# One batch's pieces reordered between another's channel products, its value casts moved to GpSimd, and three batches' numerators placed a step earlier (attention and MLP mixer)

## The chip, the cores and the metric

One core of a Trainium2 chip runs the whole kernel. The metric is the device time of one execution in microseconds (us); the time of a version is the median of its runs.

## The reference

Eight batches of eight heads, 576 positions, 64 features per head. Linear attention with cosine and sine weights is followed by a mixer that has a token part and a channel part:

```python
q_p, k_p = phi(q, cos_w, sin_w), phi(k, cos_w, sin_w)   # relu(x)*cos, relu(x)*sin
kv  = einsum('bhsf,bhsd->bhfd', k_p, v)
num = einsum('bhsf,bhfd->bhsd', q_p, kv)
den = einsum('bhsf,bhf->bhs', q_p, sum_s(k_p))[..., None] + 1e-06
x   = num / den                                         # heads side by side: (8, 576, 512)
h   = relu(x^T @ w_tok1) @ w_tok2                       # token part
u   = x + h^T
out = u + relu(u @ w_ch1) @ w_ch2                       # channel part
```

## The kernel before

**Tiles.** The 576 positions of a batch are four chunks of 128 (numbers 0 to 3) and a tail of 64; the tails of an even and the next odd batch share one tile of 128 partitions (`Tail`). `R` is 4, so "chunk `R`" is the tail; `NCH` is 12, the blocks of the hidden channel width.

**Two parts of a batch.** `Front` computes everything up to `u`, `Channel` the channel part. The order is written out by hand (manual schedule): each engine runs its instructions in the order in which the Python code issues them, and waits on semaphores where data or a buffer is missing. The channel part of batch b is a list of steps: 12 steps `c` (a block of `u @ w_ch1`, four matmuls of 512 columns; slots 0 to 11, from `C` = 0), then steps of two matmuls each for `o` (the product with `w_ch2`; slots from `O` = 12). Behind each step, `pieces` puts pieces of the front part of batch b+1, by a plan of (slot, function, arguments); within a slot they run in the order of the plan. So TensorE's own stream is: a step, some pieces, a step, some pieces.

**The pieces.** `KS` and `QS` (k_side, q_side) make the cosine and the sine product of a chunk of keys or queries (line 264 on VectorE; with `True` the sine goes to ScalarE, line 262). `QT` (q_trans) turns a chunk of queries on TensorE (line 343, eight transposes into a PSUM tile of pool `ps_at`, which has two buffers) and copies it out on ScalarE (line 347) or VectorE (line 349); later batches turn by DMA instead (line 353). `V` (values, line 267) casts a chunk of values to bf16 into `v_aug`. `KV` (line 321) multiplies keys and values of a chunk into `kv_ps` (one `ps_at` buffer), `kv_out` (line 332) copies the sum out, one half on ScalarE and the other on VectorE. `N` (num, line 362, `num_ps` in `ps_at`) gives numerator and denominator of a chunk; three VectorE instructions divide. `mix_head` and `mix_tail` are the first token product (line 385, relu at lines 390 and 392), `T` (tok2) is the second (line 409) with the addition that makes `u` (line 412) and its cast (lines 414, 416). `u_trans_dma` and `tail_trans_dma` turn `u` by DMA from SP's queue (lines 438, 443) for the next channel part. Stores of finished outputs are issued from SP too (line 571).

**The first two batches.** The front part of batch 0 (`first_front`) runs alone. The channel part of batch 0 starts before batch 0's `u` has been added up, so the five `tok2` calls of batch 0 (`before.tok2`) are among the pieces of batch 1. Batch 1's plan has its own branch (`first`) and ends in one long slot 11, in which the rest of its front work up to `kv_out` is issued between the last `c` and the first `o`.

**Loads.** SP issues all loads of queries, keys and values in a written order; GpSimd issues the weights `w_ch1` and `w_ch2` (line 194).

Of the kernel before, what the change touches and what calls it, by code (L numbers as in the profile page):

```python
# [16 lines left out]
def kernel(  # L17
# [15 lines left out]
    nc = tc.nc  # L33

    B, H, S, D = q.shape
# [5 lines left out]
    R = S // P  # L41
    SM = R * P
    ST = S - SM
    NSC = R + 1
    NCC = Dm // P
    NT = D_tok // P
    NCH = D_ch // P
# [9 lines left out]
    def half(g):  # L57
        return slice(g * ST, (g + 1) * ST)
# [14 lines left out]
    ps_at = ctx.enter_context(tc.tile_pool(name="ps_at", bufs=2, space=bass.MemoryType.PSUM))  # L73
# [14 lines left out]
            in_=src[b, lo:hi, 0:SM, :].rearrange("h (p r) d -> p h r d", r=R))  # L88


    def load_tail(dst, src, b):
        return nc.sync.dma_start(out=dst[half(b % 2)],
                                 in_=src[b, :, SM:S, :].rearrange("h s d -> s h d"))

    def tiles():
# [8 lines left out]
    load_main(qt0, q, 0, 0, HH)  # L104
    load_main(qt0, q, 0, HH, H, nc.scalar)
    load_tail(qtt0, q, 0)
    load_main(kt0, k, 0, 0, HH)
    k_done = load_main(kt0, k, 0, HH, H)
    load_tail(ktt0, k, 0)
    load_main(vt0, v, 0, 0, HH)  # L110
    load_tail(vtt0, v, 0)
    load_main(vt0, v, 0, HH, H)

# [72 lines left out]
    for c2 in range(2):  # L186
        for ki in range(0, NCC, 2):
            w_ch1_done.append(nc.gpsimd.dma_start(
                out=w_ch1[:, ki:ki + 2, c2 * C2:(c2 + 1) * C2],
# [27 lines left out]
    class Front:  # L217
# [243 lines left out]
        def pieces(self, b, before):  # L461


            first, odd = b == 1, b % 2 == 1
            V, KV, N = self.values, self.kv, self.num
            KS, QS, QT, T = self.k_side, self.q_side, self.q_trans, self.tok2
            C, O = 0, NCH
            if first:

                last = NCH - 1  # L470
                plan = [(4, KS, 0), (5, KS, 1, True), (6, KS, 2, True), (6, KS, 3, True), (7, KS, R),
                        (8, QS, 0), (9, QS, 1), (9, QT, 0), (10, QS, 2), (10, QT, 1)]
                plan += [(last, *what) for what in (
                    (QS, 3, True), (QT, 2, (0, H), nc.vector), (before.tok2, 2, None, False),
                    (QS, R, True), (QT, 3), (before.tok2, 3, None, False),
                    (QT, R, (0, H), nc.vector), (before.tok2, R, None, False))]
                plan += [(last, V, ci, eng) for ci, eng in enumerate(
                    (nc.gpsimd, nc.gpsimd, nc.scalar, nc.scalar, nc.vector))]
                plan += [(last, KV, ci) for ci in range(NSC)]
                plan.append((last, self.kv_out))  # L480
                plan += [(5, before.tok2, 0, ps_at, False), (7, before.tok2, 1, ps_at, False)]
            else:
                plan = [(C + at, V, ci, nc.scalar) for ci, at in enumerate((-1, -1, 0, 1, 2))]
                plan += [(C + at, KS, ci) for ci, at in enumerate((0, 0, 1, 2, 2))
                         if ci < R or not odd]
                for ci, at in zip(ORDER, (1, 2, 3, 4, 5)):
                    if ci < R or not odd:
                        plan += [(C + at, QS, ci), (C + at, self.q_trans_dma, ci)]

                plan += [(C + at, KV, ci) for ci, at in  # L490
                         enumerate((2, 3, 4, 5, 6) if odd else (2, 3, 4, 6, 7))]
                plan.append((C + (6 if odd else 7), self.kv_out))
            if first:
                at, mix, t = (O + 1, O + 3, O + 5, O + 7, O + 9), O + 10, O + 14
            elif odd:
                at, mix, t = (C + 8, C + 9, C + 11, O + 1, O + 3), O + 4, O + 8
            else:
                at, mix, t = (C + 9, C + 10, C + 11, O + 1, O + 3), O + 4, O + 8
            plan += [(i, N, ci) for i, ci in zip(at, ORDER)]
            plan += [(mix, self.mix_head, 0), (mix + 1, self.mix_head, 1),  # L500
                     (mix + 2, self.mix_tail)]

            plan += [(t + at, T, ci) for ci, at in enumerate((0, 1, 2, 3, 3) if not first else
                                                             (0, 0, 1, 2, 2))]
            plan += [(t + 3 - first, self.u_trans_dma, 3, R)]
            plan.append((t + 2 - first, self.u_trans_dma, 0, 3))
            if odd:
                plan.append((t + 3 - first, self.tail_trans_dma))
            slots = {}
            for slot, what, *args in sorted(plan, key=lambda p: p[0]):  # L510
                slots.setdefault(slot, []).append((what, args))
            return slots
# [269 lines left out]
```

## Time and profile before

| | us |
|---|---|
| median of 3 runs (276.20 to 278.07) | 277.34 |
| profiled execution, device time | 275.45 |
| its span (first to last instruction) | 273.60 |
| TensorE busy in the span | 261.6 |
| VectorE, ScalarE, GpSimd busy | 164.7, 129.8, 11.2 |

The profile is of one execution. "Busy" of TensorE is modelled from the matmuls' starts; a matmul of 512 columns is listed with 372 ns, but the next one starts 216 ns after it (24 of them start between 24.10 and 29.28 us), so 216 ns is what one costs where TensorE is never idle. A "wait" is idle time of an engine in front of an instruction, with the engine or transfer that ended it. A time with a colon or without a unit is a place in the span, in us from its start. The granted TensorE clock is 1.00 over the whole span.

By time, the span falls into the lone front part of batch 0 (0 to 24), the channel part of batch 0 with batch 1's pieces (24 to 60), then one channel part of about 30 us per batch, and the last one alone (from 244).

### The profile page before, as it was taken

What the parts mean: (1) busy time and instruction counts of PE and PEld (TensorE: products, weight loads), DVE (VectorE), ACT (ScalarE), POOL (GpSimd) and SP (SyncE); (2) the same over time, 40 slices, a digit from 0 to 9 for tenths busy, and PEclk for the clock granted to TensorE, in tenths of its full rate; (3) what the DMA queues carried; (4) which work ended last, traced back from release to release, by engine and by line L of the source; (5) the groups of instructions that cost most, each with busy time, mean ns of one, the idle gap of its engine ahead of it and who ended that gap; (6) DMA issues with size and microseconds to landing.
All of it is one profiled execution on the core that took longest, in us unless ns stands there. A gap on an engine that the chain in (4) does not pass through costs nothing.

```text
span 273.6 us, 5130 instructions
## 1 busy us (share of the span) xinstructions
PE 261.6 (96%) x2050; PEld 138.7 (51%) x2050; DVE 164.7 (60%) x375; ACT 129.8 (47%) x229; POOL 11.2 (4%) x24
## 2 busy tenths in 40 slices
PE   7989987999899999999999999999999999999994
PEld 2665354446554454445654455446644455435543
DVE  6973775774876396659566487659466577720022
ACT  4955982067525184156626183347606372426500
POOL 6400230000000000000000000000000000000000
PEclk9999999999999999999999999999999999999999
DMA  7999999738995897968993969669994361180032
GB/s 222 344 266 283 317 179 283 245 88 264 284 253 185 247 221 191 323 140 233 208 311 79 270 193 259 220 151 237 211 304 119 115 117 38 42 210 0 2 98 94
DMA packets 91816, 53.68 MB, mean 196 GB/s; under 512 B 59409, under 2 KB 86929, under 8 KB 91793
## 3 DMA queue, kind: packets, MB, share of 16 engines
q1 hardware_dynamic: 88432, 49.62, 65.4%
q0 software_dynamic: 2832, 3.21, 7.1%
q10 hardware_dynamic: 528, 0.52, 0.6%
q8 instruction: 16, 0.26, 0.4%
q14 instruction: 8, 0.06, 0.1%
HBM read 35.85 MB, written 9.44 MB: 166 GB/s over the span
## 4 chain that ended last, share of the span: by engine, by line
PE 80%; DMA 7%; DVE 7%; ACT 2%; issue 1%; SPq 0%; DVEq 0%
PE o_ps L564 31%; PE c_ps L531 23%; PE b_ps L385 6%; PE u_ps L409 5%; PE num_ps L362 4%; PE ct_ps L551 4%; DMA qpT<-qp 4%; PE kv_ps L321 3%; DVE qp L264 2%; DMA uT<-u_bf 2%; DMA qt<-in_q_dram 2%; DVE kp L264 2%; PE idle_ps L205 1%; PE c_ps L541 1%; DVE u_sb L412 1%
## 5 line engine op out<-in xcount | busy, mean ns | idle before, releaser
L564 PE MATMUL o_ps<-w_ch,h1T 128*128 128x512 bf16 (+1 forms) x396 | 94.8, 372 | 0.0
L531 PE MATMUL c_ps<-uT,w_ch 128*128 128x512 bf16 (+2 forms) x384 | 91.6, 372 | 1.0 <-DMA uT<-u_bf 1.0
L535 ACT ACTIVATE h1T<-c_ps 128x512 bf16<-128x512 f32 x93 | 55.4, 598 | 57.1 <-PE c_ps L531 56.9
L564 PEld LDWEIGHTS <-h1T 128*128 128x128 bf16 x396 | 37.0, 97 | 38.8
L531 PEld LDWEIGHTS <-w_ch 128*128 128x128 bf16 x384 | 33.3, 97 | 31.2 <-DMA uT<-u_bf 2.0
L569 DVE TENSOR_TENSOR o_sb<-o_ps,u_sb 128x512 f32<-128x512 f32 (+1 forms) x33 | 22.2, 673 | 32.7 <-PE o_ps L564 32.7
L412 DVE TENSOR_TENSOR u_sb<-u_ps,x_sb 128x512 f32<-128x512 f32 x32 | 22.0, 689 | 7.3 <-PE u_ps L409 6.8
L416 ACT CAST u_bf<-u_sb 128x512 bf16<-128x512 f32 x28 | 17.3, 618 | 17.8 <-DVE u_sb L412 16.1
L390 ACT ACTIVATE B<-b_ps 128x512 bf16<-128x512 f32 x8 | 4.8, 597 | 39.5 <-PE b_ps L385 39.5
L409 PE MATMUL u_ps<-B,w_tok 128*128 128x512 bf16 x80 | 22.5, 379 | 0.0
L372 DVE TENSOR_TENSOR x_sb<-num_ps,den 128x512 bf16<-128x512 f32 x28 | 19.4, 691 | 1.0
L551 PEld LDWEIGHTS <-w_ch 128*128 128x128 bf16 x192 | 14.0, 98 | 9.2
L264 DVE TENSOR_SCALAR qp<-qt,cos_t 128x512 bf16<-128x512 f32 (+1 forms) x35 | 15.9, 453 | 4.6 <-DMA qt<-in_q_dram 4.6
L385 PE MATMUL b_ps<-x_sb,w_tok 128*128 128x512 bf16 x64 | 17.9, 379 | 0.0
L264 DVE TENSOR_SCALAR kp<-kt,cos_t 128x512 bf16<-128x512 f32 x32 | 15.2, 480 | 3.9 <-DMA kt<-in_k_dram 3.9
L551 PE MATMUL ct_ps<-uT_tail,w_ch 128*128 128x128 bf16 x192 | 17.2, 219 | 0.0
L275 ACT CAST v_aug<-vt 128x512 bf16<-128x512 f32 (+1 forms) x30 | 16.7, 586 | 0.1
L264 DVE TENSOR_SCALAR qp<-qt,sin_t 128x512 bf16<-128x512 f32 (+1 forms) x34 | 15.7, 460 | 0.0
L362 PEld LDWEIGHTS <-qpT 128*128 128x128 bf16 x256 | 11.5, 98 | 7.1 <-DMA qpT<-qp 1.5
L362 PE MATMUL num_ps<-kv_sb,qpT 128*128 128x65 bf16 x256 | 13.1, 193 | 1.7 <-DMA qpT<-qp 0.7
L569 DVE TENSOR_TENSOR o_sb<-o_ps,u_tail 128x512 f32<-128x512 f32 x4 | 2.8, 692 | 20.0 <-PE o_ps L564 20.0
L321 PE MATMUL kv_ps<-v_aug,kp 128*128 128x65 bf16 x256 | 12.5, 193 | 2.2 <-ACT v_aug L275 1.7
(96 smaller groups left out, 220.9 us busy)
## 6 DMA issues: line engine op xcount, KB each, us to landing
out_dram<-o_sb SPq DMA_DIRECT2D x31, 256.0 KB, 2.9
kt<-in_k_dram SPq DMA_DIRECT2D x7, 1024.0 KB, 6.9
qt<-in_q_dram SPq DMA_DIRECT2D x7, 1024.0 KB, 8.6
vt<-in_v_dram SPq DMA_DIRECT2D x7, 1024.0 KB, 6.5
w_ch<-in_moe_w_ch_dram POOLq DMA_DIRECT2D x4, 384.0 KB, 10.4
w_ch<-in_moe_w_ch_dram POOLq DMA_DIRECT2D x3, 512.0 KB, 8.3
out_dram<-o_sb SPq DMA_DIRECT2D x10, 128.0 KB, 2.3
qtt<-in_q_dram SPq DMA_DIRECT2D x8, 128.0 KB, 5.9
```

Of the source, the lines that this page charges most:

```text
L264: nc.vector.tensor_scalar(o_ap, i_ap, scalar1=w, scalar2=0.0, op0=ALU.mult, op1=ALU.max)
L321: nc.tensor.matmul(self.kv_ps[g][:, j * DP:j * DP + D1], self.k_of(ci)[:, g * HH + j, :, :] .rearrange("p a b -> p (a b)"), self.va[:, ci, ...
L362: nc.tensor.matmul(num_ps[:, g, j * DP:j * DP + D1], self.qT_of(ci, h), self.kv_sb[g][:, j, 0:D1], start=True, stop=True)
L372: nc.vector.tensor_mul(self.x_of(ci)[rows].rearrange("p (g j d) -> p g j d", g=2, j=HH), nv[:, :, :, 0:D], den.to_broadcast([rows.stop - r ...
L385: nc.tensor.matmul(self.b1_ps[mi], w, self.x_of(ci), start=(ci == ORDER[0]), stop=(ci == ORDER[-1]))
L409: nc.tensor.matmul(u_ps, w_tok2[:, ki, ci * P:(ci + 1) * P], self.B1[:, ki, :], start=(ki == 0), stop=(ki == NT - 1))
L412: nc.vector.tensor_add(u, u_ps[rows], self.x_of(ci)[rows])
L531: nc.tensor.matmul(c_ps[:, lo:hi], w_ch1[:, ki, mi * P:(mi + 1) * P], uT[:, lo // P:hi // P, ki, :], start=(ki == 0), stop=(ki == NCC - 1))
L535: nc.scalar.activation(self.h1T[:, mi, :], c_ps, AF.Relu)
L551: nc.tensor.matmul(self.ct_ps[:, mi % R, :], w_ch1[:, ki, mi * P:(mi + 1) * P], self.tail.uT[:, ki, :], start=(mi % R == 0 and ki == 0), s ...
L564: nc.tensor.matmul(o_ps, h, w_ch2[:, ki, cols], start=ki == 0, stop=ki == NCH - 1)
L569: nc.vector.tensor_add(o_sb, o_ps, u)
```

## The change

Three things are changed. First, in batch 1's plan: the second `tok2` of batch 0 goes from slot 7 to slot 8, behind one more `c` block; the query pieces go one slot later; in slot 11 the third and fourth `tok2` each stand between two transposes, the sine product of query chunk 3 goes from ScalarE to VectorE, the copy of its transpose from ScalarE to VectorE, and the tail's `tok2` goes to the end, behind the key-value products. Second, the value casts of chunks 2 and 3 of batch 1 go from ScalarE to GpSimd, which had chunks 0 and 1. Third, in batches 3, 5 and 7 the numerators of chunk 2, of the tail and of chunk 3 stand one step earlier (slots C+10, C+11, O+2 instead of C+11, O+1, O+3), and with them both token products and the transposes of `u`; the store of the output chunk that is finished in between, so far issued between the two transposes of `u`, is then issued behind both.

`load_tail` gets a parameter for the issuing engine; no call passes it, and the loads keep their engine and their order.

```diff
-    def load_tail(dst, src, b):
-        return nc.sync.dma_start(out=dst[half(b % 2)],
+    def load_tail(dst, src, b, eng=nc.sync):
+        return eng.dma_start(out=dst[half(b % 2)],
                                  in_=src[b, :, SM:S, :].rearrange("h s d -> s h d"))
...
             if first:
-                last = NCH - 1
-                plan = [(4, KS, 0), (5, KS, 1, True), (6, KS, 2, True), (6, KS, 3, True), (7, KS, R),
-                        (8, QS, 0), (9, QS, 1), (9, QT, 0), (10, QS, 2), (10, QT, 1)]
-                plan += [(last, *what) for what in (
-                    (QS, 3, True), (QT, 2, (0, H), nc.vector), (before.tok2, 2, None, False),
-                    (QS, R, True), (QT, 3), (before.tok2, 3, None, False),
-                    (QT, R, (0, H), nc.vector), (before.tok2, R, None, False))]
-                plan += [(last, V, ci, eng) for ci, eng in enumerate(
-                    (nc.gpsimd, nc.gpsimd, nc.scalar, nc.scalar, nc.vector))]
-                plan += [(last, KV, ci) for ci in range(NSC)]
-                plan.append((last, self.kv_out))
-                plan += [(5, before.tok2, 0, ps_at, False), (7, before.tok2, 1, ps_at, False)]
+                dve, every, u = nc.vector, (0, H), before.tok2
+                plan = [(4, KS, 0), (5, KS, 1, True), (5, u, 0, ps_at, False), (6, KS, 2, True),
+                        (7, KS, 3, True), (7, KS, R), (8, u, 1, ps_at, False), (9, QS, 0),
+                        (9, QS, 1), (10, QT, 0), (10, QS, 2), (11, QT, 1), (11, QS, 3),
+                        (11, QS, R, True), (11, u, 2, None, False), (11, QT, 2, every, dve),
+                        (11, u, 3, None, False), (11, QT, 3, every, dve), (11, QT, R, every, dve)]
+                plan += [(11, V, ci, nc.gpsimd) for ci in range(R)]
+                plan.append((11, V, R, dve))
+                plan += [(11, KV, ci) for ci in range(NSC)]
+                plan += [(11, self.kv_out), (11, u, R, None, False)]
...
             elif odd:
-                at, mix, t = (C + 8, C + 9, C + 11, O + 1, O + 3), O + 4, O + 8
+                at, mix, t = (C + 8, C + 9, C + 10, C + 11, O + 2), O + 3, O + 7
```

## The prediction

> **What bounds the kernel now.** I read the busy times first, then the table of 5 us windows, then TensorE's timeline in the windows that are not full, and there the timelines of the engine that ended each wait.
>
> ```profile
> PE 261.6 (96%) x2050; PEld 138.7 (51%) x2050; DVE 164.7 (60%) x375; ACT 129.8 (47%) x229; POOL 11.2 (4%) x24
> ...
> 30.00:35.00 5.00, 4.32 (x27) 2.06 (x26) 4.60 (x10) 4.34 (x8) 2.41 (x3) 1.00 1.02 266
> 35.00:40.00 5.00, 4.35 (x44) 2.59 (x41) 3.40 (x8) 4.85 (x7) 1.47 (x3) 1.00 1.14 184
> 40.00:45.00 5.00, 3.23 (x55) 2.15 (x53) 2.58 (x5) 2.62 (x5) 0.00 (x0) 1.00 1.14 240
> ...
> 240.00:245.00 5.00, 4.39 (x21) 1.88 (x20) 1.38 (x2) 0.08 (x2) 0.00 (x0) 1.00 0.66 169
> ```
>
> After the window's bounds and length come the busy us of TensorE, its weight loads, VectorE, ScalarE and GpSimd. TensorE is full (5.00) in nearly every window from 75 to 240. No matmul is added or removed, so the change can only win idle time: 0.68 + 0.65 + 1.77 = 3.10 us between 30 and 45, 1.56 between 60 and 75, 0.61 at 243.8, 0.13 at 105. Which instructions wait:
>
> ```profile
> 34.44 0.62 PE L343 MATMUL qT_ps<-ident,qp 128*128 128x128 bf16 x8 [0.68 <-DVE qp L264]
> 38.76 0.62 PE L343 MATMUL qT_ps<-ident,qp 128*128 128x128 bf16 x8 [0.65 <-ACT qp L262]
> 42.95 0.92 PE L321 MATMUL kv_ps<-v_aug,kp 128*128 128x65 bf16 x16 [1.65 <-ACT v_aug L275]
> 243.80 2.76 PE L531 MATMUL c_ps<-uT,w_ch 128*128 128x512 bf16 x12 [0.61 <-DMA uT<-u_bf]
> ```
>
> The largest is the values: ScalarE casts chunks 2 and 3 only at 42.29, behind the tail's `u` (the in-order queue, not the cast, is late). GpSimd did its two casts six us earlier. The timelines of GpSimd and VectorE (start, us, instruction), then the instructions of the tile `vt` (shortest, median, longest in ns):
>
> ```profile
> 36.11 1.40 POOL L277 CAST v_aug<-vt 128x512 bf16<-128x512 f32 x2 [1.04 <-DMA vt<-in_v_dram]
> ...
> 36.01 0.47 DVE L264 TENSOR_SCALAR qp<-qt,cos_t 128x512 bf16<-128x512 f32 x1
> 1.90 0.99 DVE L142 TENSOR_SCALAR theta<-theta 128x5 f32<-128x5 f32 x1
> 1.92 0.95 POOL L181 MEMSET kp_tail<- 64x1024 bf16 x1
> ```
>
> ```profile
> L277 POOL CAST v_aug<-vt x2: 608/724/840, 36.1 to 36.9; 128x512 bf16<-128x512 f32 x2
> ```
>
> These matter for the cost. The first cast (0.840) began beside a VectorE product and took 0.23 longer than the second (0.608), which had VectorE idle beside it. A VectorE operation on five columns took 0.99 and ended at 2.89, two hundredths after a GpSimd memset that started beside it; its neighbour on the same tile took 0.171.
>
> **First part: the new order, without any meeting of VectorE and GpSimd.** Durations are those of before; the order on each engine is that of the built program.
> - The second `tok2` starts behind one more `c` block (four matmuls of 0.216), at 32.30 instead of 31.44. From the start of two such matmuls to VectorE's addition it is 0.64 (234.39 to 235.03), so that starts at 32.94 instead of 32.77, and all products behind it are 0.17 later. Chunk 0's sine ended at 34.38 and now ends at 34.55; TensorE has blocks until 34.46. The wait of 0.68 shrinks to 0.15.
> - TensorE then runs QT0 34.6, block 11 35.05, QT1 35.91, `tok2` 36.35, QT2 36.78, `tok2` 37.22 (0.44 for eight transposes, 0.43 for a `tok2`), and would be at QT3 at 37.65. Its PSUM buffer is that of QT1, whose copy (1.01, ScalarE, behind block 11's relu) ends there: QT3 at 37.7.
> - VectorE, which now has the sine of chunk 3 (0.39) and QT3's copy: cosine 3 at 36.18, sine 36.57, tail cosine 36.97, addition 37.36, QT2's copy 37.97, addition 38.58, QT3's copy 39.19 to 39.88 (0.39 from one product's start to the next, 0.61 for the others).
> - QTR takes QT2's buffer (38.7), and `kv_ps` QT3's, free at 39.88. So KV starts at 39.9, not for values but for PSUM. In before 24 KV matmuls took 1.00 (42.95 to 43.95), so 40 take 1.67: 41.57. The tail's `tok2` ends at 42.0, and the first `o` starts there instead of at 43.95: 1.95 won. That `tok2` also covers `kv_out`, for which the first numerators waited about 0.1 (0.35 for eight instead of 0.24): 2.05 in all.
>
> The values hide there: four casts of 0.608 from 36.11 end at 38.5, or of 0.840 at 39.5; the last is needed at 40.9. If the load (9.2 from issue to landing) came later still by 1.4, that cover would be gone. The `w_ch2` pieces were issued at 32.59, 33.34 and 34.15; with 6.2, 8.3 and 10.4 to landing they are there at 38.8, 41.6 and 44.5, needed at 42.0, 44.3 and 46.5.
>
> **Second part: casts against products.** GpSimd has four casts instead of two from 36.11 on, and VectorE has three products left (cosine 3, sine 3, tail cosine), where before it had one under way and then sat idle until 37.72. No row shows several products behind several casts. If a product waits for a cast as the theta row waited, it costs 0.6, and each moves the chain that ends in QT3's copy and KV. Bounds: nothing, or 3 x 0.6 = 1.8 if they take turns; below nothing is excluded, since a cast does no product's work. Both rows nearest to it show waiting, so I take two to three turns, 1.5. The first part is then worth 2.05 - 1.5 = 0.55 (0.25 to 2.05).
>
> The Trainium skill (SBUF — State Buffer, section "Who interferes with whom") states such a rule, and it speaks against this change: VectorE in a two-port mode and GpSimd lock each other out for a whole instruction, and whoever starts first wins. By it all three products wait, and the sum would be 0.25 here; the theta row (0.99) and the longer cast (0.840) agree with it.
>
> **Third part: batches 3, 5, 7 a step earlier.** A step is two matmuls, 0.43. Only batch 7 has idle time to win. Before, `u`'s second transpose was issued at 241.23, behind a store (240.27) that waited for an output addition which VectorE ran ahead of `u`; its 2.5 to landing ended the wait of 0.61 at 243.80. Now the cast of chunk 2 ends at 237.67 instead of 238.10, the first transpose takes SP 2.05 as before, the second follows at 239.85 and lands at 242.35, while `o` lasts until 243.19. All 0.61 goes. The store is queued behind three transposes, some 3 us later, with four output buffers.
>
> The price: chunk 2's numerators stand 0.86 earlier (a `c` block) and need their turned queries. Issue plus time to landing: batch 3 102.56 + 3.7 = 106.26 against 106.32 needed; batch 5 162.33 + 2.8 = 165.1 against 166.5; batch 7 223.43 + 2.8 = 226.2 against 226.75. That fits with 0.06 to spare in batch 3. I charge 0.05: 0.55. The relu on VectorE (0.69) behind an output addition now ends about when the second `tok2` matmul wants it (both near 234.2), free.
>
> **Sum.** 0.55 + 0.55 = 1.1 us of the profile's 273.60 us span; the profiled execution took 275.45, 1.85 around it. The median is 1.89 above that execution, in places the profile can't show; taking the gain off the median: 277.34 - 1.1 = 276.2.
>
> What is next late: the 1.56 between 60 and 75, all behind the third batch's queries (issued 61.30, 6.0 to landing) and `u`'s transposes (57.21). These follow batch 1's `u` in SP's queue, so they move with it. The loads of before issued from 41.74 to 48.34 don't move; SP's first store was at 50.63, now about 49.
>
> **Rivals.**
> 1. *No turns.* VectorE's products go back to back (0.39 apart, 0.47 long, so they overlap), and GpSimd gets in only behind them, or the values land later than 36.1. For: it has finished 38.5 + 1.2 = 39.7 in time. Against: the two rows. Gain 2.05 + 0.6 = 2.65: 274.7. Longer waits than the profile's in the typical execution (its 1.89) would add to it.
> 2. *The gain is swallowed.* TensorE comes to 60 earlier, but the third batch's queries land no earlier, because SP or the transfers (busy 1.1 in the window 45 to 50) hold them; the words of the change speak of loading them right behind the turned `u`, but no load moves, so here it does not do what it says. Against: DMA share 0.36 in 55 to 60. Only the last 0.6 stays: 276.7.
> 3. *Slower: numerators wait for turned queries.* At slot C+10 in batches 3, 5 and 7. Transposes took 2.7 to 5.6 to land; at 5.6 the three would stall 1.8, 1.4 and 2.3 = 5.5, less 1.1: 281.7. It decides from 0.4 us of stall per batch on. For: 0.06 to spare. Against: those over 4.4 stand at 68 to 72 and at 126.7, in even batches, and batches 5 and 7 have 1.4 and 0.55 spare.
>
> **How the numbers follow.** Turns 0.44 (276.2; alone 275.2 to 277.0), no turns 0.31 (274.7), swallowed 0.13 (276.7), slower 0.12 (281.7 at its end, 278 to 282). Within 1% means 274.57 to 280.11, about what a measurement of this kernel can tell from no change. Rival 1 lies at that edge: three quarters of it, 0.23, go to faster, and 0.02 of turns. Half of rival 3 is over the other edge: 0.06, and 0.01 for noise. The range: from 274.0 (rival 1 with the runs' spread of about 0.7 below it) to 277.4 (swallowed with the same); it leaves out rival 3 and some 0.07 at the ends.
>
> **What would show it.** Right: GpSimd casts and VectorE products alternating from 36, products of 0.9 to 1.1; KV starting between 41 and 41.6, its wait ended by a VectorE copy and no longer by ScalarE's cast; no wait in front of the last channel part. Rival 1: KV at 39.9. Rival 2: more than 1.6 idle between 58 and 75. Rival 3: numerators waiting for `qpT` near 106, 166 or 226. I am wrong altogether if the values land after 39 or TensorE loses its clock.

## The result and the profile after

| us | before | changed |
|---|---|---|
| median of 20 runs each | 277.42 (276.01 to 278.71) | 275.99 (274.37 to 277.49) |
| profiled execution, device time | 275.45 | 274.87 |
| its span | 273.6 | 273.1 |
| TensorE busy | 261.6 | 260.9 |
| first `c` block, KV, first `o` | 24.10, 40.63, 43.95 | 24.23, 41.85, 43.57 |
| last channel part | 243.80 | 243.26 |

The ratio of the times is 0.9945, 95% interval 0.9924 to 0.9967: by the medians the changed kernel is 1.4 us faster. The gain is small, but the interval leaves 1 out. The two profiled executions differ by only 0.6, because the one of before lies below the lowest of its 20 timed runs (275.45 against 276.01).

The windows of 5 us of the changed kernel, in the columns of the prediction:

```profile
30.00:35.00 5.00, 4.77 (x23) 1.96 (x22) 4.31 (x9) 4.69 (x9) 2.38 (x3) 1.00 1.01 285
35.00:40.00 5.00, 3.94 (x39) 2.48 (x41) 4.94 (x9) 3.60 (x5) 2.86 (x4) 1.00 1.15 183
40.00:45.00 5.00, 3.71 (x63) 2.75 (x64) 4.03 (x8) 0.45 (x2) 0.00 (x0) 1.00 1.10 233
...
240.00:245.00 5.00, 5.00 (x25) 2.27 (x24) 1.38 (x2) 0.60 (x1) 0.00 (x0) 1.00 0.67 179
```

Between 30 and 45 TensorE is now idle for 0.23 + 1.06 + 1.29 = 2.58 instead of 3.10, and the last window is full. ScalarE's column has fallen from 2.62 to 0.45 in the third window: the values and the copy of the fourth transpose (1.13 and 0.58 in that window of before) are no longer there, and the cast of the tail's `u` comes later. VectorE's has risen from 3.40 to 4.94 of 5.00 in the second. TensorE's timeline shows who ends its waits:

```profile
34.98 0.62 PE L343 MATMUL qT_ps<-ident,qp 128*128 128x128 bf16 x8 [0.23 <-DVE qp L264]
...
38.81 0.62 PE L343 MATMUL qT_ps<-ident,qp 128*128 128x128 bf16 x8 [0.45 <-DVE qp L264]
40.65 0.61 PE L343 MATMUL qT_ps<-ident,qp_tail 128*128 128x128 bf16 x8 [1.21 <-DVE qpT L349]
41.85 1.15 PE L321 MATMUL kv_ps<-v_aug,kp 128*128 128x65 bf16 x32 [0.59 <-DVE qpT L349]
...
43.57 1.03 PE L562 MATMUL o_ps<-w_ch,h1T 128*128 128x512 bf16 x4
```

Every wait is now ended by VectorE, the last two by its copies, which free the PSUM buffers. VectorE was held up here:

```profile
34.10 0.82 DVE L264 TENSOR_SCALAR qp<-qt,sin_t 128x512 bf16<-128x512 f32 x1
34.84 0.47 DVE L264 TENSOR_SCALAR qp<-qt,cos_t 128x512 bf16<-128x512 f32 x1
35.23 0.47 DVE L264 TENSOR_SCALAR qp<-qt,sin_t 128x512 bf16<-128x512 f32 x1
35.63 0.88 DVE L264 TENSOR_SCALAR qp<-qt,cos_t 128x512 bf16<-128x512 f32 x1
36.43 0.83 DVE L264 TENSOR_SCALAR qp<-qt,sin_t 128x512 bf16<-128x512 f32 x1
37.18 0.83 DVE L264 TENSOR_SCALAR qp<-qt,cos_t 128x512 bf16<-128x512 f32 x1
37.93 0.83 DVE L264 TENSOR_SCALAR qp<-qt,sin_t 128x512 bf16<-128x512 f32 x1
```

The casts on GpSimd beside them, from its timeline, and in ns (shortest, median, longest) from the view of `vt`:

```profile
35.62 2.86 POOL L277 CAST v_aug<-vt 128x512 bf16<-128x512 f32 x4 [0.94 <-DMA vt<-in_v_dram]
```

```profile
L277 POOL CAST v_aug<-vt x4: 611/802/807, 35.6 to 37.7; 128x512 bf16<-128x512 f32 x4
```

The two products in front of the first cast, which starts at 35.62, take 0.47 (the one at 34.10 is taken up in the last section). The four behind take 0.83 to 0.88 and start 0.75 to 0.80 apart, and three of the four casts take 0.8 instead of 0.61. They take turns, as the prediction said, but there are four meetings, not two to three, and a turn costs about 0.75 - 0.39 = 0.36, not 0.6.

At the end, SP's queue and TensorE's last channel part:

```profile
237.92 3.36 SPq L438 DMA_TRANSPOSE uT<-u_bf  x2
241.72 1.20 SPq L443 DMA_TRANSPOSE uT_tail<-ub_tail  x1
243.02 1.50 SPq L569 DMA_DIRECT2D out_dram<-o_sb  x3
```

```profile
243.26 2.75 PE L529 MATMUL c_ps<-uT,w_ch 128*128 128x512 bf16 x12
```

Both transposes of `u` now stand together, the stores behind them, and the last channel part starts without a wait.

### The profile page after: what moved, and what is told of

It is laid out like the page before. It is cut to its first block, busy times and chain, and to the rows that moved or that the text cites. A ratio compares the mean times of both kernels' runs of the same rounds, so it can differ in the third digit from the quotient of the medians.

```text
span 273.1 us, 5108 instructions
## 1 busy us (share of the span) xinstructions
PE 260.9 (96%) x2029; PEld 139.3 (51%) x2050; DVE 167.5 (61%) x377; ACT 127.0 (47%) x225; POOL 12.9 (5%) x26
## 4 chain that ended last, share of the span: by engine, by line
PE 80%; DVE 11%; DMA 7%; issue 1%; DVEq 0%
PE o_ps L562 32%; PE c_ps L529 22%; PE b_ps L385 6%; PE u_ps L409 6%; DVE qp L264 4%; DMA qpT<-qp 4%; PE ct_ps L549 4%; PE num_ps L362 3%; PE kv_ps L321 3%; DVE x_sb L372 2%; DMA qt<-in_q_dram 2%; DMA uT<-u_bf 1%; DVE kp L264 1%; PE idle_ps L205 1%; PE c_ps L539 1%
## 5 line engine op out<-in xcount | busy, mean ns | idle before, releaser
L562 PE MATMUL o_ps<-w_ch,h1T 128*128 128x512 bf16 (+1 forms) x382 | 93.1, 372 | 0.6
L409 PE MATMUL u_ps<-B,w_tok 128*128 128x512 bf16 x77 | 21.9, 379 | 0.3
L264 DVE TENSOR_SCALAR qp<-qt,cos_t 128x512 bf16<-128x512 f32 (+1 forms) x35 | 16.7, 476 | 4.7 <-DMA qt<-in_q_dram 4.7
L264 DVE TENSOR_SCALAR qp<-qt,sin_t 128x512 bf16<-128x512 f32 (+1 forms) x35 | 16.9, 484 | 0.0
L275 ACT CAST v_aug<-vt 128x512 bf16<-128x512 f32 (+1 forms) x28 | 15.6, 584 | 0.1
```

The costliest lines, as they stand in the source:

```text
L264: nc.vector.tensor_scalar(o_ap, i_ap, scalar1=w, scalar2=0.0, op0=ALU.mult, op1=ALU.max)
L409: nc.tensor.matmul(u_ps, w_tok2[:, ki, ci * P:(ci + 1) * P], self.B1[:, ki, :], start=(ki == 0), stop=(ki == NT - 1))
L562: nc.tensor.matmul(o_ps, h, w_ch2[:, ki, cols], start=ki == 0, stop=ki == NCH - 1)
```

## The experiments

The theory: the new order is worth about two us, the meetings on GpSimd take most of it back, and the third part wins the wait at the end. The rivals: the casts alone, not the order, win the first part; and in the third part it is the place of the store, not the earlier step, that counts. All kernels compute the whole reference.

Two measures are used. *d* is the time from the first `c` block to the first `o` in the profiled execution. The other is needed because the times of most kernels fall into two clusters: each timed run lists its mean granted TensorE clock, and of the 51 runs of before in the three later sessions 27 have 0.998 to 1.0 and a mean of 276.81, 24 have 0.992 to 0.994 and a mean of 278.50. So I give, beside the ratio of the times (which is not the quotient of the medians), the mean of the runs at full clock (0.997 and over), and how many runs were below it; these means are good to some 0.1 to 0.2. The changed kernel has 275.10 at full clock, with 11 of its 20 runs below. What brings the clock down is in the last section.

| kernel | ratio to before, 95% | full clock: mean, before in that session | runs below | d |
|---|---|---|---|---|
| before, its two profiles | 1 | | 24 of 51 | 19.85, 20.27 |
| changed | 0.9945 (0.9924 to 0.9967) | 275.10 | 11 of 20 | 19.34 |
| e1, parts one and two | 0.9960 (0.9932 to 0.9987) | 275.62, 276.67 | 7 of 12 | 18.96 |
| e2, part three | 0.9958 (0.9931 to 0.9986) | 275.91, 276.67 | 5 of 12 | 20.10 |
| e3, changed, casts on ScalarE | 0.9838 (0.9810 to 0.9866) | 273.33, 276.67 | 0 of 6 | 17.67 |
| e4, part two | 0.9913 (0.9883 to 0.9942) | 275.41, 276.67 | 0 of 6 | 18.68 |
| e6, before, store behind | 0.9963 (0.9935 to 0.9991) | 275.85, 276.95 | 6 of 12 | 20.62 |
| e7, e3 + early queries | 0.9847 (0.9804 to 0.9889) | 273.13, 276.95 | 1 of 6 | 17.80 |
| e8, e3, transposes first | 0.9845 (0.9813 to 0.9877) | 273.56, 276.95 | 0 of 6 | 18.00 |
| e9, e3 once more | 0.9843 (0.9807 to 0.9879) | 273.40, 276.81 | 0 of 6 | 17.75 |
| e10, e7 and e8 together | 0.9888 (0.9835 to 0.9942) | 272.77, 276.81 | 4 of 6 | 18.00 |
| e11, parts two and three | 0.9887 (0.9856 to 0.9918) | 274.50, 276.81 | 0 of 6 | 18.46 |
| e12, e3, store behind in place of part three | 0.9845 (0.9813 to 0.9877) | 273.33, 276.81 | 0 of 6 | 17.63 |

**e1: the first two parts without the third.** The changed kernel with

```diff
-                at, mix, t = (C + 8, C + 9, C + 10, C + 11, O + 2), O + 3, O + 7
+                at, mix, t = (C + 8, C + 9, C + 11, O + 1, O + 3), O + 4, O + 8
```

> The new plan of batch 1 with all values on GpSimd, and batches 3, 5, 7 as before. Theory A (products and casts take turns): from the load of the values on, VectorE's products start about 0.75 us apart instead of 0.39; KV starts near 41.8, the first o near 43.5; 0.4 to 0.6 us won there, and the wait of about 0.6 in front of the last channel part stays, so the time is 0.3 to 0.6 us under before. Rival B (the products are slow for another reason, and the stage wins nothing that lasts): no difference from before. Rival C (the whole gain of 1.4 is here, the profiled execution being a poor sample): 1.2 us or more under before.

At full clock it is 1.05 under before, more than the 0.3 to 0.6 that I expected and near rival C. d is 1.1 under the mean of three executions with the old order and the old casts (19.85, 20.27, e2 20.10: 20.1). The fourth, e6, is left out: in its profile the granted clock is 0.50 from 44.2 on, in front of its first `o`, and up to KV it takes what the second profile of before takes (16.95). TensorE's timeline has the wait at the end again:

```profile
244.15 1.04 PE L529 MATMUL c_ps<-uT,w_ch 128*128 128x512 bf16 x4 [0.96 <-DMA uT<-u_bf]
```

**e2: the third part alone.** Before with the opposite edit.

> Only batches 3, 5 and 7 a step earlier. Theory A: the wait in front of the last channel part (0.61 in before, at 243.8) is gone, numerators of chunk 2 in batch 3 wait at most 0.2 for their turned queries; 0.4 to 0.7 us under before. Rival: the earlier numerators wait for turned queries in batches 3, 5, 7 as much as is won: no difference, with such waits near 106, 166 or 226.

It is 0.76 under before at full clock (0.4 to 0.7 expected), and its last channel part starts without a wait. With e1 that makes 1.81; the changed kernel is 1.71 under the pooled 276.81 (for the runs of before beside it no clock is recorded). The parts add up.

**e3: the changed kernel with the value casts on ScalarE.** It tells what the meetings cost.

```diff
-                plan += [(11, V, ci, nc.gpsimd) for ci in range(R)]
+                plan += [(11, V, ci, nc.scalar) for ci in range(R)]
```

> The changed kernel, but the casts of value chunks 0 to 3 on ScalarE instead of GpSimd, in the same place of the plan. Theory A (casts on GpSimd hold VectorE's products up): products back at 0.39 apart through 35 to 38, the copy of the fourth transpose ends near 40.1 instead of 41.8, KV starts there, the first o near 42.2 instead of 43.57: 1.2 to 1.5 us under the changed kernel, 2.2 to 2.9 under before. ScalarE's four casts of 0.55 behind the tail's sine end near 41. Rival B (products slow for another reason): products stay at 0.75 apart and the time equals the changed kernel's or is worse, since ScalarE's casts come later.

VectorE's timeline at the same place as above, then ScalarE's:

```profile
35.43 0.47 DVE L264 TENSOR_SCALAR qp<-qt,cos_t 128x512 bf16<-128x512 f32 x1
35.83 0.47 DVE L264 TENSOR_SCALAR qp<-qt,sin_t 128x512 bf16<-128x512 f32 x1
36.22 0.47 DVE L264 TENSOR_SCALAR qp<-qt,cos_t 128x512 bf16<-128x512 f32 x1
36.62 0.47 DVE L264 TENSOR_SCALAR qp<-qt,sin_t 128x512 bf16<-128x512 f32 x1
```

```profile
38.71 2.18 ACT L275 CAST v_aug<-vt 128x512 bf16<-128x512 f32 x4
```

The products are back at 0.47, 0.39 apart. The casts take 2.18 on ScalarE, and KV still waits for a PSUM buffer and not for them:

```profile
40.19 1.15 PE L321 MATMUL kv_ps<-v_aug,kp 128*128 128x65 bf16 x32 [0.59 <-DVE qpT L349]
41.24 0.40 PE L321 MATMUL kv_ps<-v_aug,kp_tail 128*128 128x65 bf16 x8
41.69 0.38 PE L409 MATMUL u_ps<-B,w_tok 128*128 128x512 bf16 x1
41.91 1.03 PE L562 MATMUL o_ps<-w_ch,h1T 128*128 128x512 bf16 x4
```

d is 17.67, and 17.75, 17.63 and 17.80 in e9, e12 and e7, which have the same order up to here: 17.71 in the mean. The changed kernel has 19.34 and e1, the same program up to here, 18.96: 19.15 in the mean. The casts on GpSimd thus cost 1.25 to 1.63, 1.44 in the mean, and four turns of 0.36 are as much. At full clock e3 is 1.77 under the changed kernel, a little over the 1.2 to 1.5 that I expected, and 3.34 under before, where I expected 2.2 to 2.9. By the medians it is 4.5 under before, since none of its runs is below full clock.

**e4: the second part alone.** Before, where only the engine of two casts changes:

```diff
-                    (nc.gpsimd, nc.gpsimd, nc.scalar, nc.scalar, nc.vector))]
+                    (nc.gpsimd, nc.gpsimd, nc.gpsimd, nc.gpsimd, nc.vector))]
```

> The kernel before with one edit: the casts of value chunks 2 and 3 on GpSimd instead of ScalarE. Theory A: in the old order VectorE has one product left when the values land, so only that one meets a cast; the wait of 1.65 in front of KV's third chunk goes, a wait for the tail's values (VectorE, near 42.2) of some 0.2 to 0.4 takes its place: first o near 42.5 instead of 43.95, 1.1 to 1.5 us under before, more than the new plan with the same casts. Rival (the new order is needed for the casts to be worth anything): the same time as before.

TensorE's timeline:

```profile
41.25 1.16 PE L321 MATMUL kv_ps<-v_aug,kp 128*128 128x65 bf16 x32
42.85 0.40 PE L321 MATMUL kv_ps<-v_aug,kp_tail 128*128 128x65 bf16 x8 [0.44 <-DVE v_aug L277]
43.09 1.03 PE L564 MATMUL o_ps<-w_ch,h1T 128*128 128x512 bf16 x3
```

The values no longer stop KV at its third chunk; 0.44 is left for the tail's values, which VectorE casts last. By the medians it is 2.5 faster, nearly twice what I expected; at full clock 1.26, which is what I expected. The rest, about 277.88 - 276.67 = 1.2, is what the runs below full clock add to the median of before; e4 had none. With casts on GpSimd the old order is not worse than the new one: d is 18.68 here and 18.46 in e11, against 18.96 and 19.34. Here three products meet casts (at 35.70, 36.47 and 37.22, 0.82 to 0.85 long) and not the one that I expected; in the new order there are four, and VectorE has the sine of chunk 3 on top.

**e5: before once more,** to see how typical its first profile was.

> The kernel before once more, for a second profile of it. Theory A (the first profile of before was a fast sample of the same code): the lone front part and the waits near 34 and 43.8 add up to some 0.5 to 1 us more than in the first, and the span is nearer to 275 than to 273.6. Rival (the medians and the profiles differ in something outside the span): the span is 273.6 within 0.2 again.

Its span is 275.2 instead of 273.6 at a full clock. Of the 1.6, 0.42 are in d and 0.45 in front of the last channel part, where the wait is 1.06; numerators of batch 3 wait 0.66 instead of 0.13. The first profile was of a short execution. TensorE's timeline:

```profile
245.40 1.90 PE L531 MATMUL c_ps<-uT,w_ch 128*128 128x512 bf16 x8 [1.06 <-DMA uT<-u_bf]
```

**e6: before, with only the store moved.** In batches 2, 4 and 6 the store of output chunk 1 (`store` issues it, `c.later` is the same call put off) is issued behind the transposes of the next batch's `u`; the steps stay.

```diff
+                if b in (2, 4, 6) and ci == 1:
+                    self.later = store
+                else:
+                    store()
...
+            if b in (2, 4, 6) and i == NCH + 11:
+                c.later()
```

> The kernel before with one edit: in batches 2, 4 and 6 the store of output chunk 1 is issued behind the transposes of u instead of between them; no piece is moved to an earlier step. Theory A (the store in SP's queue made the wait of 0.6 to 1 in front of the last channel part): u's second transpose is issued at once behind the first, lands about 1 us earlier, and the wait shrinks to 0.2 or less: 0.4 to 0.9 us under before, as much as the earlier steps won. Rival (the step of 0.43 is what counts): more than half of the wait stays.

SP's queue and TensorE's timeline:

```profile
241.35 3.22 SPq L438 DMA_TRANSPOSE uT<-u_bf  x2
245.00 1.20 SPq L443 DMA_TRANSPOSE uT_tail<-ub_tail  x1
```

```profile
246.25 1.03 PE L531 MATMUL c_ps<-uT,w_ch 128*128 128x512 bf16 x4
```

The wait is gone with the steps as they were, and at full clock the kernel is 1.10 under before, at least what the whole third part wins. So the store between the two transposes was the cause, and the earlier step is not needed.

**e7, e8 and e10: can e3 be bettered?** e7 loads the third batch's queries right behind its keys and values, since TensorE waits for them at 65 to 75; e8 puts the transposes of chunks 2 and 3 in front of their `tok2`; e10 does both. **e9** is e3 again.

```diff
-                load_batch(2, "kv", behind=w_ch2_done[1])
-            if b == 0 and i == NCH + 16:
-                load_batch(2, "q")
+                load_batch(2, "kvq", behind=w_ch2_done[1])
```

```diff
-                        (11, QS, R, True), (11, u, 2, None, False), (11, QT, 2, every, dve),
-                        (11, u, 3, None, False), (11, QT, 3, every, dve), (11, QT, R, every, dve)]
+                        (11, QS, R, True), (11, QT, 2, every, dve), (11, u, 2, None, False),
+                        (11, QT, 3, every, dve), (11, u, 3, None, False), (11, QT, R, every, dve)]
```

> The changed kernel with the value casts on ScalarE and, beside that, the third batch's queries loaded right behind its keys and values (from about 48) instead of behind u's transposes. Theory A (the waits of about 1.1 to 1.3 us in the second channel part are this load's landing): no wait for kp or qpT between 60 and 75; 0.8 to 1.3 us under the same kernel with the late load (273.4 by the last measurement), so about 272.3. Rival (the transfers of that stage only change places: the load holds up stores or u's transposes): 273.4 or more, with a longer wait for uT near 59.

> The changed kernel with the value casts on ScalarE and, beside that, the third and fourth transpose each in front of the tok2 that stood in front of them. Theory A (VectorE's queue of products, additions and copies sets where KV starts): one addition of 0.6 fewer lies ahead of the copy of the fourth transpose, KV starts 0.4 to 0.6 earlier, of which a wait for ScalarE's last value cast takes 0.2 to 0.4: 0.1 to 0.5 us under the same kernel in the old order (273.4). Rival (PSUM or ScalarE sets it): no difference.

> The changed kernel with the value casts on ScalarE, once more, beside its variants in one session. Theory A: 3 to 5 us under before again (ratio 0.982 to 0.988), VectorE's products 0.39 apart, first o 17.5 to 18.1 after the first block of c. Rival (the first result was a lucky set of runs): ratio 0.990 or more.

> Value casts on ScalarE, transposes in front of their tok2, and the third batch's queries loaded right behind its values. Theory A (each of the two takes a wait away and another comes in its place: ScalarE's last cast for KV; the transposes of u, held up by the earlier load, in front of the second channel part): within 0.6 us of the kernel with the casts on ScalarE alone. Rival (they add up): 0.8 us or more under it.

Neither edit won anything that can be told: 273.13 and 273.56 at full clock, against 273.33 and 273.40 for e3 and e9. In e7 the windows from 65 to 75 are full, where e3 has 0.28 + 1.31 idle. But in front of batch 1's channel part the wait for `u`'s transposes, 0.43 in e3, is longer, as TensorE's timeline says:

```profile
59.71 2.46 PE L529 MATMUL c_ps<-uT,w_ch 128*128 128x384 bf16 x18 [1.29 <-DMA uT<-u_bf]
```

In e8 KV is stretched from 1.15 to 1.63, since ScalarE's casts now come too late; TensorE's timeline, then ScalarE's:

```profile
40.28 1.63 PE L321 MATMUL kv_ps<-v_aug,kp 128*128 128x65 bf16 x32 [0.32 <-DVE qpT L349]
```

```profile
39.28 2.18 ACT L275 CAST v_aug<-vt 128x512 bf16<-128x512 f32 x4
```

The last cast ends at 41.46, while in e3 it ended at 40.89. e10 was the plain miss: I expected it within 0.6 of e9, and its median is 2.0 longer (its ratio in the table leaves out its longest run). It waits 2.01 at the same place as e7, and four of its six runs are below full clock (275.14 to 276.20); the two others are 272.09 and 273.45. That early queries lengthen this wait is seen twice (1.29 and 2.01); by which queue they do so was not told apart.

**e11: parts two and three with the old order.** The edits of e4 and e2 together.

> The kernel before with all value casts of batch 1 on GpSimd and batches 3, 5, 7 a step earlier, but the old order of batch 1's pieces. Theory A (in the old order fewer products stand in front of what KV waits for, so the casts cost less there): 3 to 3.6 us under before (2.4 and 1.1 measured for the two parts), and 1.5 us or more under the changed kernel, so the new order takes time as long as the casts are on GpSimd. Rival (the parts overlap, or the new order is worth something): 1.5 us under before or less.

At full clock it is 2.31 under before, near the 1.26 + 0.76 = 2.02 of its parts; by the medians it is 2.6 and by the ratio 3.1, where I expected 3 to 3.6. By the ratios it beats the changed kernel too (0.9887 against 0.9945, the intervals apart): next to these casts the new order is a loss. At full clock the loss is 0.6 here and 0.2 between e1 and e4, the latter no more than the means are good to; the rest of it are the runs below full clock.

**e12: e3 with e6's store in place of the third part.**

> The new plan of batch 1 with the value casts on ScalarE, batches 3, 5, 7 in their old steps, and the store between the transposes of u issued behind them instead. Theory A (the store made the wait in front of the last channel part, the earlier steps are not needed): no wait there, within 0.6 us of the kernel with the casts on ScalarE and the earlier steps. Rival (the earlier steps are worth something of their own): 0.8 us or more over it.

273.33, as e3 to the hundredth, and no wait in front of the last channel part. The versions with the casts on ScalarE, e10 aside, lie furthest under before: by the ratios 1.5 to 1.6%, where the changed kernel is 0.55% under it.

## Why the prediction was right

The time is 0.2 under the forecast, and the case that came is "turns".

1. **The new order without meetings, 2.05.** e3 shows it by itself: first `o` at 41.91, with a first `c` block 0.14 later than in the first profile, so 41.77 against the 42.0 forecast; KV at 40.05 against 39.9. d is 2.1 under the first profile of before and 2.4 under the mean of the three. The step holds, for the reason given: KV waits for PSUM and no longer for values.
2. **Meetings take back 1.5.** They take 1.44 in the mean. The total is right by luck, since both factors were wrong and the errors cancelled: four products met casts (the values landed at 35.62, not 36.1, when both products of chunk 2 were still to come), at 0.36 each. The theta row (0.99) was the wrong neighbour. The longer cast of before's own trace was nearer: it was 0.23 late, and its sisters here are 0.19 late.

   The Trainium skill's rule (SBUF — State Buffer, "Who interferes with whom") has the direction right: the two engines hold each other up, and on ScalarE the same casts disturb no product. The size that the prediction drew from it does not agree. If each waited for the whole listed length of the other's instruction, a pair of product and cast would take 0.39 + 0.61 = 1.0; the pairs take 0.75. Four meetings at 0.6 would have cost 2.4, more than the 2.05 that the order wins. For how much of its listed length an instruction holds the other engine up, the traces do not show, so the rule itself is not refuted.
3. **What is left of the first part: 0.55 forecast, 1.05 measured** (e1 at full clock; 20.1 - 19.15 = 0.9 by d). The step is the base: the sum was made against the first profile, in which d is 0.25 and 0.42 shorter than in the two others of that order at full clock. Against that profile the changed kernel's d is 0.51 under, but e1's is 0.89 under with the same program up to there, so that the near agreement with 0.55 is luck too.
4. **The third part, 0.55.** 0.76 (e2), for the same reason: the wait that goes is 0.61 in the first profile and 1.06 in e5. I had put it down to the earlier step and the store's place together; e6 and e12 show that the store alone does it.
5. **Numerators behind turned queries** (the 0.05 charged, rival 3). None of the moved ones waits. One in batch 3 waits longer than before in TensorE's timeline, but it stands at C+9, a slot that wasn't moved:

```profile
105.35 0.42 PE L362 MATMUL num_ps<-kv_sb,qpT 128*128 128x65 bf16 x8 [0.77 <-DMA qpT<-qp]
```

   It waits 0.13 in before's first profile and 0.66 in e5, with no change at all: the time to landing varies from one execution to the next.
6. **Rivals.** "No turns" falls: products and casts alternate. "Swallowed" falls, if narrowly by the sign that the prediction gave it (more than 1.6 idle between 58 and 75): TensorE is idle there for 1.58, but before has 1.56 and 1.63 in its two profiles, so the new order's gain did not go into waits there.
7. **KV between 41 and 41.6, products of 0.9 to 1.1.** KV came at 41.85 and the products at 0.83 to 0.88: both just outside, by the sizes in 2.

The forecast gain of 1.1 against 1.4 (medians) or 1.7 (full clock) is thus mostly the low base of 3 and 4; the mechanism of each step holds, though not the factors of 2. The 1.89 by which the median of before lay above its profiled execution, and which the prediction carried over unexplained, now divides: 276.81 - 275.45 = 1.36 is the short execution, and the rest are runs below full clock. Carrying it over worked because the changed kernel has about as many of these (11 of 20 against 24 of 51). The prediction did not ask for that; for e4, which has none, taking 1.26 off the median of before beside it would have missed by 1.2.

## What to carry over

Before work goes to an idle engine, look which engine it will hold up there: the casts went to an engine that had time, and held up the one that was on the chain; ScalarE, which had become free by the very reorder, did them at no cost that reached TensorE. Profile the kernel before twice before gains of half a microsecond are worked out from one execution. And where a wait is ended by a transfer, look at what stands in front of it in its queue: one store, issued one place later, won as much as moving all the steps.

## What the hardware showed that I had not expected

**The granted clock fell to half for 3.4 us behind stretches in which TensorE was about half busy.** Three windows of e6, whose profiled run is one of those below full clock (0.994), in the same columns; the granted clock is the third number from the end:

```profile
40.80:44.20 3.40, 1.63 (x32) 1.03 (x29) 2.05 (x4) 2.13 (x4) 0.00 (x0) 1.00 1.15 232
44.20:47.60 3.40, 3.18 (x29) 2.02 (x30) 0.62 (x3) 0.38 (x1) 0.00 (x0) 0.50 1.12 340
47.60:51.00 3.40, 3.40 (x38) 1.98 (x37) 3.01 (x9) 0.00 (x0) 0.00 (x0) 1.00 1.10 323
```

And of e10 (0.992), around its wait of 2.01:

```profile
58.20:61.60 3.40, 1.39 (x8) 0.53 (x7) 2.36 (x6) 0.81 (x2) 0.00 (x0) 1.00 0.98 182
61.60:65.00 3.40, 3.40 (x14) 1.73 (x13) 3.40 (x10) 0.00 (x0) 0.00 (x0) 0.50 0.71 189
```

Half the clock for 3.4 us loses 1.7 where TensorE is the bound, and 1.7 of 276 is a mean clock of 0.994: the two clusters of before are 1.69 apart and show that clock. Which kernels have the second cluster goes with their emptiest 3.4 us (windows as long as the drop, after the first `c` block, in steps of half a microsecond up to 88 and of one behind; one profile of each kernel). The windows of before, of the changed kernel and of e3 there:

```profile
41.00:44.40 3.40, 1.63 (x37) 1.20 (x34) 1.15 (x3) 1.90 (x4) 0.00 (x0) 1.00 1.13 228
```

```profile
38.50:41.90 3.40, 1.28 (x18) 1.03 (x19) 3.34 (x7) 0.39 (x1) 0.00 (x0) 1.00 1.21 198
```

```profile
37.00:40.40 3.40, 2.28 (x33) 1.79 (x33) 3.34 (x7) 3.35 (x6) 0.00 (x0) 1.00 1.20 190
69.00:72.40 3.40, 2.09 (x23) 1.28 (x22) 2.01 (x6) 1.68 (x3) 0.00 (x0) 1.00 1.26 195
```

Where TensorE is busy for 1.28 to 1.67 of it (before, changed, e1, e2, e6, e10), 57 of 113 runs are below full clock; where it is busy for 2.09 or more (e3, e4, e8, e9, e11, e12), none of 36; e7 (2.08) has one of six. So the change left the drop as likely as it was (11 of 20 against 24 of 51), while moving the casts alone, or to ScalarE, took it away, and that is the part of their median gains that the waits don't explain. The profiled executions at full clock with 1.28 and 1.63 show that the stretch alone does not decide it. The line between the two groups was drawn after the fact, and no run varied the stretch by itself. The lone front part, left out above, has emptiest windows of 1.84 (e9, 4.5 to 7.9) to 2.03, with no drop behind them in any trace.

The Trainium skill (TensorE: Matmul & The Clock Gate, "What's actually happening") describes such a gate: half rate after an idle window of about 3.4 us, with windows that run free of the kernel. The half rate, the 3.4 us and the chance from run to run agree with the rows above. "Idle", taken as no work at all, does not: TensorE was busy for 1.63 and 1.39 of the 3.4 before these drops, and its longest wait in them was 2.01. That the phase of such windows decides which runs are hit fits, and was not tried by itself.

**A meeting costs both engines.** Beside a product, a cast on GpSimd takes 0.80 instead of 0.61; beside a cast, a product takes 0.83 instead of 0.47, and a pair goes through in 0.75. The sine product at 34.10, while GpSimd issued a load of `w_ch2` (33.91, 0.76 long), took 0.82 too, with no cast beside it. In e1, where GpSimd had issued the last of these loads by 34.14, the same product (34.31) took 0.47, and its d is 0.38 shorter than that of the changed kernel: the 0.35 of this one product is about the difference between the two.
